# Attention rows loaded in three pieces, zero-padded queries loaded in place, and a longer first lead

## The chip, the cores and the metric

The kernel runs on one core of a Trainium2 chip. The metric is the device time of one execution in microseconds (us). PE is the matrix engine (TensorE), PEld its weight loads, DVE the vector engine, ACT the scalar engine, POOL the GpSimd engine, SP the engine that issues nearly all DMAs here. A name followed by q (SPq, ACTq) is an engine's queue of instructions.

## The reference, cut to what matters

```python
# q, k, v: (4 batches, 8 heads, 576 positions, 64), float32
scores = scale * q @ k.T                                  # per batch and head
Dmat   = where(i >= j, gamma[h] ** (i - j), 0)            # decay mask, gamma[h] = 1 - 2**(-5 - h)
x      = (scores * Dmat) @ v                              # to (2304 tokens, 512)
h      = x @ w_in                                         # dense layer, 512 -> 2048
x      = (h * sigmoid(1.702 * h)) @ w_out                 # 2048 -> 512
expert = argmax(normalised x . normalised expert_emb / tau)   # one of 8 experts per token
out    = gate * relu(x @ w1[expert]) @ w2[expert]         # 512 -> 1024 -> 512
```

## The kernel before

Three stages follow one another: attention (to about 79 us of the profiled span), the dense layer on six blocks of 384 tokens (to about 490 us), and the experts. Only attention and the first microseconds of the dense layer are touched.

**Tiling of attention.** Two heads make a pair; 4 batches by 4 pairs give 16 pairs `bp`. A pair's 576 positions are four chunks of 128 and a tail of 64, so 80 steps `(bp, ch)` in all, `ch` 4 being the tail. A recurrent state `kvs` carries what earlier chunks contribute: within a step PE computes the scores of the chunk (L298, or L301 for the tail), adds the chunk to the state (L325; ACT scales it out of PSUM in L327), and forms the output from the state (L341, from chunk 1 on) and from the masked scores `pr` (L345). DVE multiplies scores by the mask (`pr`, L303) and the finished output by a decay (`keep`, L363 and L360).

**Data of a pair.** `att[bp]` is one row buffer of 128 partitions by 2048 floats (1 MB): columns 0 to AK=512 are the keys transposed (K), AK to AV=1024 the keys in natural order, AV to AQ=1536 the values, AQ to AW=2048 the queries. There are five row buffers (`NBUF`). The matmuls read the queries from a tile `qz` (four of them, `NQ`), in which each head's queries stand in its own 64 partitions and the other 64 partitions are zero; the zeros are written once at the start (L278). `tails[b]` holds, for the four pairs of a batch, the tail's keys, queries and values (384 KB). `tab` holds masks and decays.

**`load(bp)`** issues the whole row as one DMA on SP, for the first batch also the pair's table, and for the first pair of a batch the tails. Pair 0 alone is different: its queries go straight from DRAM into `qz[0]` beside the zeros, in two DMAs, one for each head, and its other columns come over ACT's queue in two pieces.

**`prep(bp)`** makes a loaded pair ready on POOL: it copies the queries of each head from the row into `qz` (L310, not for pair 0), scales the natural keys by a decay (L313; on DVE for pair 0), and copies the tail's queries from `tails` into `qz` (L316, two copies).

**Order.** The instruction order is written out by hand. Odd and even pairs alternate step by step: `turns[0]` are the even pairs' steps, `turns[1]` the odd ones'. The first three steps of pair 0 go ahead, then one odd step and one even step in turn. At step i the loop issues: `prep(bp + 2)` when ch is 0; the scores of step i + 2; state and output of step i; `keep` when ch is 3 or 4; and, when ch is 4, `load(bp + 5)` into the buffer that pair `bp` leaves. At three of these places a first-layer weight unit `wd` (1 MB) is loaded too, and after the last row the constants and more `wd` units. SP issues in program order, and a DMA that waits for a buffer holds back those behind it.

**Weight conversion.** The dense weights come as 64-bit floats; a generator `convert()` turns unit after unit into two 32-bit words: ACT takes the magnitude (L165), DVE does two passes of about 0.7 us (L178, L180) and two of 1.2 us (L185, L192), ACT copies the high word (L168), and DVE subtracts it (`low`, L172). The generator yields a cost after each DVE piece. From attention step 37 on each step calls `flush()` (issue postponed ACT pieces) and `pull(0.23)` (issue pieces until that budget is spent; the overdraft is carried on as `debt`). In the dense layer `swish` pulls 2.6 within each step.

**Dense start.** The order of the first dense matmul groups on PE is h0 and h1 (unit 0 on token blocks 0 and 1), h2 (unit 1, block 0), then the second layer of h0, and so on.

Of the kernel before, what the change touches and what calls it, by code (L numbers as in the profile page):

```python
# [17 lines left out]
P = 128  # L18
B, H, S, HD = 4, 8, 576, 64
NPAIR = H // 2  # L20
NCH = 4
TAIL = S - NCH * P
# [19 lines left out]
RING = 12  # L42
BIG = 100000.0
LAG = 2
WARM = 34
HOLD = NF1 - LAG - 1 - KD
STOP = 1000.0
WD_AT = (7, 11, 14)
NWD = 3
NBUF, NQ = 5, 4  # L50
# [4 lines left out]
AK, AV, AQ, AW = NCH * P, 2 * NCH * P, 3 * NCH * P, 4 * NCH * P  # L55
TQ, TV, TAW = TAIL, 2 * TAIL, 3 * TAIL
# [18 lines left out]
def retention_moe_kernel(  # L75
# [18 lines left out]
    PE, ACT, DVE, POOL, SP = nc.tensor, nc.scalar, nc.vector, nc.gpsimd, nc.sync  # L94
# [26 lines left out]
    def unit_tile(name, shape, dt, s):  # L121
        return pool.tile(shape, dt, tag=f"unit{s % NF1}", bufs=1, name=name)
# [8 lines left out]
    def load_wd(u):  # L131

        t = unit_tile(f"wd{u}", [P, 2048], I32, HELD + u)
        stg["d", u] = t.rearrange("p (n two) -> p n two", two=2)
        SP.dma_start(t, wd[u].bitcast(I32))
# [6 lines left out]
    def load_due():  # L142

        if st.get("loaded"):
            while due:
                load_wd(due.pop(0))

    def flush(*keys):
        for k in keys or list(later):
            if k in later:  # L150
                later.pop(k)()
# [74 lines left out]
    def slot(name):  # L226
        st["slots"] = st.get("slots", -1) + 1
        assert st["slots"] < HELD
        return unit_tile(name, [P, 2048], F32, st["slots"])

    def attention():
        psum = tc.tile_pool(name="psum_a", bufs=1, space=bass.MemoryType.PSUM, reuse_waits="tile")
        with psum as psum:
            yield from attention_(psum)

    def attention_(psum):


        row = [slot(f"row{i}") for i in range(1, NBUF)]
        row.insert(0, slot("row0"))  # L240
        qz = [slot(f"qz{i}") if i > 1 else pool.tile([P, 2048], F32, tag="tab", bufs=2, name=f"qz{i}") for i in range(NQ)]
        tb = slot("tb")[:, : NPAIR * TW].rearrange("p (n w) -> p n w", w=TW)
        ends = slot("ends")
        tl = [ends[:, NPAIR * TAW * i : NPAIR * TAW * (i + 1)].rearrange("p (n w) -> p n w", w=TAW) for i in range(2)]
# [3 lines left out]
        x0[0], x0[1] = x0_tile(0), x0_tile(1)  # L248
        NBP = B * NPAIR

        def load(bp):
            t = row[bp % NBUF]
            b, pair = divmod(bp, NPAIR)
            if bp:
                SP.dma_start(t, att[bp])
            else:
                for j in range(2):
                    r = slice(64 * j, 64 * j + 64)
                    SP.dma_start(qz[0][r, S * j : S * j + NCH * P], att[bp, r, AQ:])
                ACT.dma_start(t[:, :AK], att[bp, :, :AK])  # L260
            if b == 0:
                SP.dma_start(tb[:, bp], tab[:, bp])
            if bp == 0:
                ACT.dma_start(t[:, AK:AQ], att[bp, :, AK:AQ])
            if pair == 0:
                SP.dma_start(tl[b % 2], tails[b])

        load(0)
        DVE.memset(ones, 1.0)
        ACT.copy(scr, ones[:, :16])  # L270

        warm = psum.tile([P, 512], F32, tag="o", bufs=2, name="warm")
        for _ in range(WARM):
            PE.matmul(warm[:, :P], ones, ones, start=True, stop=True)
        scs = [psum.tile([P, 512], F32, name=f"sc{i}") for i in range(3)]
        for i in range(NQ):
# [2 lines left out]

            if i < 3:  # L280
                DVE.memset(scs[i][:, : 2 * P], 0.0)
        for bp in range(1, NBUF):
            load(bp)
        POOL.memset(cum, 0.0)

        def scores(n):
# [16 lines left out]
            DVE.tensor_tensor(pr[:, :, :w], sc[:, :, :w], mask[:, :, :w], ALU.mult)  # L303

        def prep(bp):
            t, end = row[bp % NBUF], tl[bp // NPAIR % 2][:, bp % NPAIR, TQ:TV]
            for j in range(2):
                r, q0 = slice(64 * j, 64 * j + 64), S * j
                if bp:
                    POOL.tensor_copy(qz[bp % NQ][r, q0 : q0 + NCH * P], t[r, AQ:])  # L310
            kd = t[:, AK:AV].rearrange("p (c e) -> p c e", e=HD)
            dec = tb[:, bp % NPAIR, TD + P : TD + P + 2 * NCH]
            (POOL if bp else DVE).tensor_tensor(kd, kd, dec.unsqueeze(2).to_broadcast(kd.shape), ALU.mult)  # L313
            for j in range(2):
                r, q0 = slice(64 * j, 64 * j + 64), S * j + NCH * P
                POOL.tensor_copy(qz[bp % NQ][r, q0 : q0 + TAIL], end[r])  # L316

        def state(bp, ch):
            t = row[bp % NBUF]
# [58 lines left out]


        turns = [[(bp, ch) for bp in range(p, NBP, 2) for ch in range(NCH + 1)] for p in range(2)]  # L380
        steps = turns[0][:3]
        for a, b in zip(turns[1], turns[0][3:] + [None] * 3):
            steps += [a, b] if b else [a]
        prep(0)
        prep(1)
        scores(0)
        scores(1)
        for i, (bp, ch) in enumerate(steps):
            if ch == 0 and bp + 2 < NBP:
                prep(bp + 2)  # L390
            if i + 2 < len(steps):
                scores(i + 2)
            if ch < NCH:
                state(bp, ch)
            chunk(bp, ch)
            if ch >= NCH - 1:
                keep(bp, ch == NCH)
            if ch == NCH:
                if bp + NBUF < NBP:
                    load(bp + NBUF)  # L400
                if bp + NBUF in WD_AT:
                    load_wd(WD_AT.index(bp + NBUF))
                if bp + NBUF + 1 == NBP:

                    st["loaded"] = True
                    SP.dma_start(c[:, :CET], cst[:, :CET])
                    SP.dma_start(c[:, CET : CET + KD * E], embt)
                    uf = pool.tile([P, P], F32, tag="cvb", bufs=1, name="uf")
                    SP.dma_start(uf, cst[:, CU:CSL])
                    load_due()  # L410
            yield
# [458 lines left out]
    def pull(us):  # L870

        k = 0
        us += debt.pop()
        while us > 0 and k < len(bg):
            cost = next(bg[k], None)
            if cost is None:
                bg.pop(k)
            elif cost == STOP:
                k += 1
                us -= 0.7  # L880
            else:
                us -= cost
        debt.append(min(us, 0.0))

    bg.append(convert())
    for i, _ in enumerate(attention()):
        if i > 36:
            flush()
            pull(0.23)
    psum = ctx.enter_context(tc.tile_pool(name="psum", bufs=1, space=bass.MemoryType.PSUM, reuse_waits="tile"))  # L890

    def fill_slots():
# [17 lines left out]
    steps = [(blk, f) for f in range(NF1) for blk in range(2)]  # L910
# [126 lines left out]
    for i in range(nd - 1):  # L1037
# [15 lines left out]
        else:  # L1053
# [4 lines left out]
            if blk < NB - 1 and f == 6:  # L1058
                split_x0(blk + 1)
        if i >= LAG:  # L1060
            dense2(i - LAG)
            u = i - LAG - (nd - NF1)
            if u == 0:
# [7 lines left out]
    while bg:  # L1071
        pull(STOP)
    for f in range(LAG + 1):
        dense2(nd - LAG - 1 + f)
    last = last_rows()
# [185 lines left out]
```

## Time and profile before

| | |
|---|---|
| three runs | 725.32, 726.46, 727.14 us; median 726.46 |
| the profiled execution | 726.2 us; its span, first to last instruction, 724.4 us |
| busy share of the span | PE 97%, PEld 91%, DVE 64%, ACT 42%, POOL 31% |
| DMA | 113.86 MB, 157 GB/s over the span |
| mean granted clock of PE | 0.997 |

All stretches and starts are microseconds from the start of the span. A PE that is busy without a gap is taken as bound by itself; the idle time of another engine costs nothing as long as PE does not wait for it. In a timeline row the first number is the start, the second the duration, and what stands in brackets is the idle time before it and what ended it.

### The profile page before, as it was taken

The page shows a single profiled execution, that of the slowest core. Times are in us where ns is not written, and L with a number is a line of the kernel's source. Part 1 is how long each engine was busy: PE and PEld are TensorE (multiplying, and loading weights), DVE is VectorE, ACT ScalarE, POOL GpSimd, SP SyncE. Part 2 cuts the span into 40 slices and gives each one's busy share as a digit, 9 for nine tenths or more (in the row PEclk, how much of TensorE's full clock was granted, in tenths as well). Part 3 has the DMA queues.
Part 4 walks back from the last instruction along what each step waited for, and adds up shares of the span by engine and source line. Part 5 has one row for each costly group of instructions (what it writes and reads, how often), then busy time and mean ns, then how long its engine had stood idle before and what let it go on. Part 6 is the DMA issues. An engine that isn't in the chain of part 4 may idle for free. (4 is left out here: it accounts for less than half of the span.)

```text
span 724.4 us, 13776 instructions
## 1 busy us (share of the span) xinstructions
PE 704.7 (97%) x5118; PEld 658.2 (91%) x5118; DVE 464.6 (64%) x1085; ACT 306.9 (42%) x586; POOL 227.3 (31%) x251
## 2 busy tenths in 40 slices
PE   7998999999999999999999999999999999999994
PEld 6988898998998998899899899989999999999994
DVE  4788788888636887674476468656564563564561
ACT  1553354544455323332332243353445545555542
POOL 4998000000000221220111102223347457466553
PEclk9999999999999999999999999999999999999998
DMA  9998999300130012200400321144678989888761
GB/s 330 373 359 306 357 356 368 84 1 0 65 114 0 1 56 76 89 1 1 132 1 1 91 84 59 59 142 129 203 188 267 238 250 265 229 267 260 241 185 61
DMA packets 53030, 113.86 MB, mean 157 GB/s; under 512 B 8146, under 2 KB 29010, under 8 KB 48736
## 3 DMA queue, kind: packets, MB, share of 16 engines
q1 hardware_dynamic: 49472, 102.71, 44.2%
q0 software_dynamic: 3200, 9.46, 3.7%
q8 instruction: 41, 0.67, 0.4%
q10 hardware_dynamic: 288, 0.79, 0.4%
q14 instruction: 29, 0.24, 0.1%
HBM read 85.09 MB, written 28.17 MB: 156 GB/s over the span
## 5 line engine op out<-in xcount | busy, mean ns | idle before, releaser
L459 PE MATMUL h<-x,unit 128*128 128x384 f32 x1152 | 217.6, 337 | 1.3 <-DVE unit L172 1.0
L459 PEld LDWEIGHTS h<-x,unit 128*128 128x128 f32 x1152 | 204.6, 188 | 9.9 <-DVE unit L172 1.3
L218 POOL TENSOR_TENSOR unit<-we,unit 128x512 fp32r<-128x512 f32 x64 | 102.4, 1607 | 116.8 <-ACT unit L216 98.5
L459 PE MATMUL eh<-xt,unit 128*128 128x336 f32 (+6 forms) x672 | 102.1, 301 | 0.2 <-DVE eg54l L504 0.2
L459 PEld LDWEIGHTS eh<-xt,unit 128*128 128x128 f32 x672 | 95.4, 188 | 0.9 <-DVE eg54l L504 0.5
L217 DVE TENSOR_TENSOR unit<-we,unit 128x512 fp32r<-128x512 f32 x64 | 56.3, 880 | 61.7 <-ACT unit L216 61.1
L216 ACT CAST unit<-we 128x1024 fp32r<-128x1024 f32 x64 | 66.8, 1046 | 27.0 <-DMA we<-we 25.5
L566 DVE CUSTOM_DVE_ANT_0 dj<-xr,en 128x512 bf16<-128x512 f32 x120 | 78.1, 698 | 0.0
L532 POOL TENSOR_TENSOR enrm<-scr,c 128x8 f32<-128x8 f32 x1 | 1.7, 1687 | 150.4 <-ACT ej L537 150.4
L298 PE MATMUL sc<-qz,row 128*64 128x128 f32 (+1 forms) x512 | 40.0, 259 | 6.4 <-issue 2.3
L303 DVE TENSOR_TENSOR pr<-sc,tb 128x256 f32<-128x256 f32 (+1 forms) x80 | 30.6, 392 | 13.8 <-PE sc L298 11.3
L298 PEld LDWEIGHTS sc<-qz,row 128*64 128x64 f32 x512 | 31.3, 145 | 8.3 <-issue 2.9
L327 ACT ACTIVATE ends<-s,tb 128x64 f32<-128x64 f32 x64 | 19.8, 314 | 35.5 <-PE s L325 32.8
L509 POOL DMA_INDIRECT out<-y,idx x24 | 24.5, 1021 | 32.0 <-ACT y L732 21.5
L345 PE MATMUL ao<-pr,row 128*64 128x128 f32 x256 | 31.1, 283 | 0.9 <-DVE pr L303 0.8
L509 POOL DMA_INDIRECT xs<-xr,slot x18 | 19.4, 1078 | 39.1 <-DVE xr L641 35.7
L626 POOL TENSOR_TENSOR cum<-cum,oh_all 128x8 bf16<-128x8 bf16 x18 | 4.9, 275 | 67.0 <-PE rk L619 65.6
L325 PE MATMUL s<-row 128*64 128x64 f32 x256 | 24.3, 229 | 0.4 <-ACT ends L327 0.4
L341 PE MATMUL ao<-qz,ends 128*64 128x128 f32 x192 | 23.4, 280 | 0.1
L345 PEld LDWEIGHTS ao<-pr,row 128*64 128x64 f32 x256 | 20.6, 142 | 2.1 <-DVE pr L303 2.0
L432 POOL TENSOR_TENSOR x<-x0s,x 128x768 fp32r<-128x768 f32 x3 | 6.1, 2049 | 48.7 <-ACT x L431 48.7
L172 DVE TENSOR_TENSOR unit<-ca,unit 128x1024 fp32r<-128x1024 f32 x16 | 19.6, 1223 | 2.8 <-ACT unit L168 2.8
(1303 smaller groups left out, 1567.1 us busy)
## 6 DMA issues: line engine op xcount, KB each, us to landing
we<-we SPq DMA_DIRECT2D x64, 512.0 KB, 4.4
wd<-wd SPq DMA_DIRECT2D x16, 1024.0 KB, 10.3
row<-att SPq DMA_DIRECT2D x15, 1024.0 KB, 7.3
xs<-fill SPq DMA_DIRECT2D x22, 257.0 KB, 11.2
xrow<-xr SPq DMA_DIRECT2D x18, 257.0 KB, 3.8
y<-yd SPq DMA_DIRECT2D x7, 512.0 KB, 4.5
x0d<-x0f SPq DMA_DIRECT2D x4, 768.0 KB, 11.2
x0s<-x0d SPq DMA_DIRECT2D x8, 384.0 KB, 6.9
```

Of the source, the lines that this page charges most:

```text
L216: ACT.copy(w[:, 0, :], t)
L217: DVE.tensor_tensor(w[:, 1, :512], t[:, :512], w[:, 0, :512].bitcast(F32), ALU.subtract)
L218: POOL.tensor_tensor(w[:, 1, 512:], t[:, 512:], w[:, 0, 512:].bitcast(F32), ALU.subtract)
L298: PE.matmul(sc[64 * i : 64 * i + 64, j, q0:], t[:, k0 : k0 + 64], q[j][:, q0:P], start=True, stop=True)
L303: DVE.tensor_tensor(pr[:, :, :w], sc[:, :, :w], mask[:, :, :w], ALU.mult)
L325: PE.matmul(s[64 * j : 64 * j + 64], t[:, AK + c0 : AK + c0 + 64], t[:, AV + c0 : AV + c0 + 64], start=ch == 0, stop=True, skip_group_chec ...
L327: ACT.activation(kvs[bp % 2][:, 64 * ch : 64 * ch + 64], s, AF.Copy, scale=tb[:, bp % NPAIR, dec : dec + 1])
L341: PE.matmul(o[64 * j : 64 * j + 64], kvs[bp % 2][:, 64 * (ch - 1) : 64 * ch], qz[bp % NQ][:, q0 : q0 + n], start=True, stop=False)
L345: PE.matmul(o[64 * j : 64 * j + 64], v, pr[:, j, :n], start=ch == 0, stop=True)
L459: PE.matmul(h, w[:, a, P * dc : P * (dc + 1)], xt[:, b, dc, :n], start=k == 0, stop=k == len(terms) - 1)
L509: i = POOL.indirect_dma_start(out=dst[:, :], out_offset=bass.IndirectOffsetOnAxis(ap=rows, axis=0), in_=src, in_offset=None, bounds_check= ...
L566: DVE.tensor_tensor_reduce(junk, r[:, :D], en[e // 4][:, e % 4, :], 1.0, 0.0, ALU.mult, ALU.add, dots[:, E * k + e : E * k + e + 1])
```

## The change

- `LEAD = 4`: the first four steps of pair 0, its whole run of full chunks, go ahead of the first odd step instead of three. Elsewhere this shifts the two interleaved sequences against each other by one step, and leaves the last four steps of pair 15 alone at the end instead of three.
- `load` takes a column range. For pairs 5 to 15 the row comes in three DMAs, issued at different steps of the pair that leaves the buffer: the queries at its chunk 0, K at its chunk 3, natural keys and values at its tail.
- The queries of pairs 0 and 1 go into `qz` beside the zeros, two DMAs each; pair 1 needs no L310 any more.
- The tail's queries of every pair go from DRAM into `qz` by two DMAs (`load_ends`, 64 partitions by 256 bytes each), in place of POOL's L316. For pairs 4 to 15 they are issued after the tail step of the pair that leaves the `qz` tile.
- The order of the initial loads on SP becomes: queries 0, table 0, queries 1, K and keys and values of row 1, table 1, ends 0, tails 0, ends 1, then rows 2 to 4 whole, each with its table and ends (2 and 3), then tails 1. Before, tails 0 came ahead of row 1.
- After attention, ahead of the dense layer, `flush()` and `pull(2.4)`: conversion pieces that were issued within the first `swish` are issued before it.

```diff
+LEAD = 4
-        def load(bp):
-            t = row[bp % NBUF]
-            b, pair = divmod(bp, NPAIR)
-            if bp:
-                SP.dma_start(t, att[bp])
-            else:
+        def load(bp, lo, hi, q=SP):
+            if lo == AQ and bp < 2:
                 for j in range(2):
                     r = slice(64 * j, 64 * j + 64)
-                    SP.dma_start(qz[0][r, S * j : S * j + NCH * P], att[bp, r, AQ:])
...
+                    SP.dma_start(qz[bp][r, S * j : S * j + NCH * P], att[bp, r, AQ:])
+                return
+            q.dma_start(row[bp % NBUF][:, lo:hi], att[bp, :, lo:hi])
...
+        def load_ends(bp):
+
+            b, pair = divmod(bp, NPAIR)
+            for j in range(2):
+                r, q0 = slice(64 * j, 64 * j + 64), S * j + NCH * P
+                SP.dma_start(qz[bp % NQ][r, q0 : q0 + TAIL], tails[b, r, pair, TQ:TV])
+
+        load(0, AQ, AW)
+        load(0, 0, AK, ACT)
+        load_tab(0)
+        load(0, AK, AQ, ACT)
...
-        for bp in range(1, NBUF):
-            load(bp)
+        load(1, AQ, AW)
+        load(1, 0, AQ)
+        load_tab(1)
+        load_ends(0)
+        load_tails(0)
+        load_ends(1)
+        for bp in range(2, NBUF):
+            load(bp, 0, AW)
+            if bp < NPAIR:
+                load_tab(bp)
+            if bp < NQ:
+                load_ends(bp)
+        load_tails(1)
...
-                if bp:
+                if bp > 1:
                     POOL.tensor_copy(qz[bp % NQ][r, q0 : q0 + NCH * P], t[r, AQ:])
...
-            for j in range(2):
-                r, q0 = slice(64 * j, 64 * j + 64), S * j + NCH * P
-                POOL.tensor_copy(qz[bp % NQ][r, q0 : q0 + TAIL], end[r])
...
-        steps = turns[0][:3]
-        for a, b in zip(turns[1], turns[0][3:] + [None] * 3):
+        steps = turns[0][:LEAD]
+        for a, b in zip(turns[1], turns[0][LEAD:] + [None] * LEAD):
...
         for i, (bp, ch) in enumerate(steps):
+            nxt = bp + NBUF
             if ch == 0 and bp + 2 < NBP:
                 prep(bp + 2)
+            if nxt < NBP and ch in (0, NCH - 1):
+                load(nxt, *((0, AK) if ch else (AQ, AW)))
             if i + 2 < len(steps):
                 scores(i + 2)
...
             if ch == NCH:
-                if bp + NBUF < NBP:
-                    load(bp + NBUF)
...
+                if nxt < NBP:
+                    load(nxt, AK, AQ)
+                if bp + NQ < NBP:
+                    load_ends(bp + NQ)
+                if nxt < NBP and nxt % NPAIR == 0:
+                    load_tails(nxt // NPAIR)
+                if nxt in WD_AT:
+                    load_wd(WD_AT.index(nxt))
...
             pull(0.23)
+    flush()
+    pull(2.4)
```

## Rows read from the trace of the kernel before

**Rows 1.** Busy time by stretch: us, engines' busy us (instructions), PE clock, DMA share, GB/s.

```profile
0.00:10.00 10.00, 6.98 (x66) 6.07 (x66) 5.99 (x14) 1.78 (x3) 1.84 (x9) 1.00 0.80 265
10.00:20.00 10.00, 7.94 (x128) 7.47 (x129) 3.33 (x9) 2.23 (x8) 7.64 (x14) 1.00 1.02 408
20.00:30.00 10.00, 10.00 (x242) 10.00 (x240) 7.33 (x19) 5.31 (x18) 9.31 (x17) 1.00 0.96 351
...
40.00:50.00 10.00, 8.56 (x187) 7.81 (x185) 8.28 (x16) 5.51 (x14) 9.37 (x15) 1.00 0.94 342
...
```

**Rows 2.** What PE waited for, 0 to 92 us: total, times, longest.

```profile
PE sc L298 <- issue: 2.3, 2, 1.6
PE sc L298 <- POOL qz L310: 2.1, 1, 2.1
PE sc L298 <- DMA qz<-att: 2.0, 2, 1.3
```

**Rows 3.** PE's timeline at the start: start, duration, line, operation.

```profile
12.16 1.36 PE L298 MATMUL sc<-qz,row 128*64 128x128 f32 x8 [2.06 <-POOL qz L310]
...
14.17 1.05 PE L298 MATMUL sc<-qz,row 128*64 128x128 f32 x8
...
15.87 1.05 PE L298 MATMUL sc<-qz,row 128*64 128x128 f32 x8
...
18.69 0.39 PE L298 MATMUL sc<-qz,row 128*64 128x128 f32 x6
```

**Rows 4.** POOL's timeline, the query copies of pairs 1 and 2.

```profile
11.50 1.27 POOL L310 COPY qz<-row 64x512 f32<-64x512 f32 x2 [2.02 <-DMA row<-att]
...
14.55 1.28 POOL L310 COPY qz<-row 64x512 f32<-64x512 f32 x2 [0.18 <-DMA row<-att]
```

**Rows 5.** ACT's timeline: one state read of the repeating pattern, first and last.

```profile
18.45 0.31 ACT L327 ACTIVATE ends<-s,tb 128x64 f32<-128x64 f32 x1 [0.57 <-PE s L325]
...
40.62 0.32 ACT L327 ACTIVATE ends<-s,tb 128x64 f32<-128x64 f32 x1 [0.57 <-PE s L325]
```

**Rows 6.** POOL's instructions by line and shape, 42 to 72 us.

```profile
L310 POOL COPY qz<-row 64x512 f32<-64x512 f32 x14 | 9.4, 669 | 1.3 <-DMA row<-att 0.7
L313 POOL TENSOR_TENSOR row<-row,tb 128x512 f32<-128x512 f32 x7 | 8.2, 1164 | 0.6
L316 POOL COPY qz<-ends 64x64 f32<-64x64 f32 x14 | 7.2, 513 | 0.4
```

**Rows 7.** DVE's timeline: a conversion pass within attention, and the dense start.

```profile
43.73 1.52 DVE L178 TENSOR_SCALAR ca<-ca 128x1024 f32<-128x1024 f32 x1 [1.38 <-ACT ca L165]
...
80.31 0.22 DVE L412 CAST ub<-uf 128x128 bf16<-128x128 f32 x1
82.63 0.56 DVE L492 SCALAR_TENSOR_TENSOR g0t<-g0t,h 128x384 f32<-128x384 f32 x1 [2.10 <-ACT g0t L490]
```

**Rows 8.** DVE's instructions by line and shape, 42 to 80 us.

```profile
L178 DVE TENSOR_SCALAR ca<-ca 128x1024 f32<-128x1024 f32 x3 | 2.9, 963 | 1.4 <-ACT ca L165 1.4
```

**Rows 9.** The same view, 82 to 130 us, in the dense layer.

```profile
L185 DVE SCALAR_TENSOR_TENSOR ca<-wd,ca 128x1024 int32<-128x1024 int32 x7 | 8.6, 1224 | 0.2
...
L178 DVE TENSOR_SCALAR ca<-ca 128x1024 f32<-128x1024 f32 x6 | 4.1, 689 | 2.1 <-ACT ca L165 2.1
```

**Rows 10.** PE's timeline at the end of attention and the start of the dense layer.

```profile
79.12 0.29 PE L345 MATMUL at<-pr,ends 128*64 128x64 f32 x4
...
85.50 2.03 PE L459 MATMUL h<-x,unit 128*128 128x384 f32 x10 [1.01 <-DVE unit L172]
```

**Rows 11.** Busy time by stretch: first loads; 8 KB rows; 2 KB rows. Columns as Rows 1.

```profile
2.00:5.50 3.50, 2.87 (x27) 2.62 (x26) 2.85 (x7) 1.12 (x2) 0.00 (x0) 1.00 0.94 276
86.00:90.00 4.00, 4.00 (x22) 3.61 (x21) 3.48 (x6) 1.94 (x3) 0.00 (x0) 1.00 1.02 427
119.00:124.00 5.00, 5.00 (x28) 4.61 (x27) 4.40 (x6) 2.55 (x4) 0.00 (x0) 1.00 1.03 397
```

**Rows 12.** DMA queue from 64 to 65 us: packets, MB, share of 16 engines.

```profile
q1 hardware_dynamic: 404, 0.40, 119.2%
```

More of the change, by code (lines that the diff above doesn't have):

```diff
@@ L249, in attention_, with load_tab, load_tails @@
         NBP = B * NPAIR
-        def load(bp):
-            t = row[bp % NBUF]
-            b, pair = divmod(bp, NPAIR)
-            if bp:
-                SP.dma_start(t, att[bp])
-            else:
+        def load(bp, lo, hi, q=SP):
+            if lo == AQ and bp < 2:
                 for j in range(2):
                     r = slice(64 * j, 64 * j + 64)
-                    SP.dma_start(qz[0][r, S * j : S * j + NCH * P], att[bp, r, AQ:])
[L260 to L268, printed above, removed]
+                    SP.dma_start(qz[bp][r, S * j : S * j + NCH * P], att[bp, r, AQ:])
+                return
+            q.dma_start(row[bp % NBUF][:, lo:hi], att[bp, :, lo:hi])
+        def load_tab(bp):
+            SP.dma_start(tb[:, bp], tab[:, bp])
+        def load_tails(b):
+            SP.dma_start(tl[b % 2], tails[b])
+        def load_ends(bp):
[7 more added lines that the diff above has]
+        load(0, AK, AQ, ACT)
         DVE.memset(ones, 1.0)
@@ L305, in prep @@
         def prep(bp):
-            t, end = row[bp % NBUF], tl[bp // NPAIR % 2][:, bp % NPAIR, TQ:TV]
+            t = row[bp % NBUF]
             for j in range(2):
                 r, q0 = slice(64 * j, 64 * j + 64), S * j
-                if bp:
+                if bp > 1:
                     POOL.tensor_copy(qz[bp % NQ][r, q0 : q0 + NCH * P], t[r, AQ:])
@@ L398, in attention_ @@
             if ch == NCH:
-                if bp + NBUF < NBP:
-                    load(bp + NBUF)
-                if bp + NBUF in WD_AT:
-                    load_wd(WD_AT.index(bp + NBUF))
-                if bp + NBUF + 1 == NBP:
+                if nxt < NBP:
[6 more added lines that the diff above has]
+                    load_wd(WD_AT.index(nxt))
+                if nxt + 1 == NBP:
                     st["loaded"] = True
```

## The prediction

> **What bounds the kernel now.** I read the table by stretches first, to find where PE is not busy. It idles 3.0 us in the first 10 us and 2.1 us in the next, not at all from 20 to 40, 1.4 us from 40 to 50 [rows 1]. In the dense layer it is busy in the whole of 86 to 90 [rows 11], and so in nearly every stretch up to 690 us. So PE sets the time, and a microsecond that attention ends earlier is a microsecond off the total, as no stage between waits for anything but PE. DMA is at a share near 1 in the same stretches of attention [rows 1]: data are a second limit, and a transfer that is put ahead pushes back another.
>
> PE's list of waits names the gaps [rows 2]. 2.0 us for the first queries are not touched: the loads in front of them stay. 2.1 us go to pair 1's query copy on POOL, whose row landed at 11.5 us [rows 4]; pair 0 still had a full chunk to do, but its scores stand behind pair 1's in PE's order. 1.0 us goes to unit 1 of the dense weights [rows 10]. 2.3 us are two stops inside a group of eight matmuls, for which the profile names no releaser.
>
> [...] And ACT's pattern, which recurs once per pair of five steps, gives the steady pace: six periods from 18.45 to 40.62 [rows 5], 3.70 us a pair or 0.74 us a step. At 40.62 there are 44 steps left, 32.5 us at that pace, to 73.1; attention's last matmul ends at 79.41 [rows 10]. So 6.3 us are lost there: 2.3 in the two stops, 4.0 elsewhere, and these are DVE's. From step 37 it has, for ten steps, eight masks of 0.42, two of 0.29, two `keep`s of 0.69 + 0.21 and conversion of 2.3 by its budget: 8.0 us against PE's 7.4.
>
> **Part 1, the start (pairs 0 and 1 in place, new order of loads, LEAD 4).** Removed: pair 1's two copies and the wait for tails 0 ahead of its row. Row 1 landed at 11.50 with 2630 KB issued up to its end and row 2 at 14.55 with 3852 KB [rows 4]: 1222 KB in 3.05 us, 410 GB/s, in order of issue. With 2246 KB up to row 1's K and values it lands near 10.6; allowing 0.2 us for the smaller pieces, 10.8. PE leaves its first chunk at 10.1 and now has pair 0's next full step, 1.70 us at the slow level [rows 3], so pair 1's scores are asked for at 11.8 and are there: the gap of 2.06 us goes.
>
> But it comes back in part two pairs on, and here I name what is late next. The bytes ahead of row 2 are the old ones plus 64 KB of ends in 256 small packets: it lands at 14.55 + 0.15 + 0.25 = 14.95 (price of the packets below), then POOL copies each half of its queries in 0.64 us, to 16.2. PE arrives at pair 2's scores between 14.8 and 16.1, as the clock rises early or late, so row 2 decides, not the clock. Before, these scores stood at 18.69 [rows 3]; now at 16.3. Of these 2.4 us one step of 0.74 is still owed, since LEAD 4 puts pair 2 a step earlier in the order. **Gain 1.6**, from 1.0 (row 2 later by 0.6) to 2.1.
>
> Next in line is POOL. From 15 us on it has per pair of batches 0 and 1 1.27 + 1.04 + about 1.1 (low halves), which is under PE's pace, but it starts at row 2's landing, and pairs 4 and 6 are needed two steps earlier against it than before. My count of its queue puts pair 6's copies 0.3 us late. **Cost 0.3**, from 0 to 1.0.
>
> **Part 2, rows in pieces.** Keys and values still wait for the output matmul of chunk 3 of the old pair, as the whole row did; only queries (by eight steps) and K (by a step and a half) go earlier. In steady state no one waits for rows, so the gain is counted at nothing. SP issues three loads and two ends for one load, four more at 0.35 to 0.5 us each, under 2 us a pair against 3.70: its waiting covers that. The new wait is that of the ends for the tail step of the pair that leaves the `qz` tile; behind it on SP stand the next pair's K and the `wd` loads, held for two steps at most, 1.5 us. POOL, which needs them, comes nine steps later. In the first pairs the ends and tails 0 land near 12.3, the tail's scores are due at 13.5.
>
> The price in DMA time: rows of 2 KB ran at 397 GB/s against 427 for 8 KB [rows 11], which makes a row in pieces about 0.15 us longer. A slice with 384 packets of 128 to 792 bytes and some 0.22 MB of 8 KB rows took 1.0 to 1.2 us [rows 12]; the 8 KB part takes 0.52 of that, so a small packet costs an engine 20 to 28 ns, and a pair's 128 ends, eight an engine, 0.2 us. Together 0.35 us a pair. Between rows 5 and 15 the queue carries 3.94 MB besides (three `wd`, two tails), 0.84 us a row; 0.84 + 2.65 + 0.2 is just PE's 3.70. **Counted at 0**, because a lead of about 4 us (row 5 should be there at 26 and is needed at 30) covers a deficit; the other end is a rival.
>
> **Part 3, L316 gone.** 7.2 of POOL's 24.8 us in these three lines from 42 to 72 us are the ends' copies [rows 6]. That is off PE's path, but DVE's conversion passes stop behind POOL: L178 took 1.52 us at 43.73 [rows 7], with POOL's L313 running in the same time, and its three in attention 0.96 each [rows 8] against 0.69 in the dense layer, where POOL rests [rows 9]. L178 is the first of five such pairs of groups; over them the eleven passes take 12.7 us against 10.3 uncontended, so 2.4 us in a stage that DVE bounds. With POOL busy for 0.71 of the time I take the same share of the collisions away, 0.7, rounded down. **Gain 0.6**, from 0 to 2.4.
>
> **Part 4, four lone steps at the end.** A lone step waits for its own state on ACT; the last two show 0.28 us each on the weight loads. One more: **cost 0.2**, from 0.1 to 0.3.
>
> **Part 5, the pull.** The budget carried over is 43 x 0.23 less the pieces' costs, -0.23, so 2.17 buys L185 of unit 2 and `low` of unit 1, 1.22 us each [rows 9]. They fill DVE's 2.10 us between 80.53 and the first swish at 82.63 [rows 7]. Unit 1 is then ready at 83.0, h2 is due at 84.5: the gap of 1.01 us before 85.50 goes [rows 10]. Late next: the first swish by 0.34, and its low half, behind L192 and the two passes of unit 3 that the pull of 2.6 now reaches, at about 87.15, where PE wants it at 87.0. **Gain 0.8**, from 0.4 to 1.0.
>
> **Sum.** 1.6 - 0.3 + 0 + 0.6 - 0.2 + 0.8 = 2.5 us, from the profiled execution's 726.2: 723.7 us. That execution lies 0.3 under the median, 726.46. What a measurement of this kernel tells from no change is 0.3%, 2.2 us: faster is under 724.3, slower over 728.6.
>
> **The rivals.**
>
> *A, the start gives it back.* The pieces ahead of row 2 go at the rate of the first loads, 276 GB/s [rows 11], 0.4 us more, POOL's delay is its upper bound 1.0, and part 3 is nothing: 1.2 - 1.0 - 0.2 + 0.8 = 0.8, **725.4**. For it: DMA share 1.02 from 10 to 20 [rows 1], so nothing can be pulled in without pushing something out. Against: the 410 GB/s of the same stretch.
>
> *B, the unnamed stops go too.* 2.3 us more [rows 2], **721.4**. For it: they stand at places in the run of instructions that the new order moves, and DMA was nearly full at both. Against: nothing in the change removes a cause that I can name.
>
> *C, slower: transfers become the bound.* The place is SP's queue of rows 5 to 15. What is left of PE's pace for a row is 2.65 us; with the lead of 4 us over 11 rows 3.0, so it decides where pieces fall under about 350 GB/s. At the 276 GB/s of the first loads, which were pieces of 2 and 4 KB as well [rows 11], a row takes 3.8 us, 11 x 1.15 - 4 = 8.6 us lost: 726.2 - 2.5 + 8.6 = **732**. Against: the first loads include the ramp from an idle queue, and the 2 KB rows at 397 were in full flow. [...]
>
> *D, uneven DVE.* With the sequences shifted, the `keep`s of an odd and an even pair fall within six steps of ten, 4.3 us of DVE work in 4.4 before any conversion piece, then four light ones. If that makes the loss of 4.0 us half again as large, **725.7**. Against: DVE is bound over the whole ten steps either way.
>
> **Chances.** The forecast 0.48, its own range 722.6 to 724.8; A 0.18, B 0.12, C 0.10, D 0.12. Faster: four fifths of the forecast's, all of B and a little of A, 0.52; slower: C and a remainder, 0.11; same 0.37. The range 721.2 to 727.4 leaves out C and the far side of B.
>
> **What would show it.** Right: PE without a wait near 10 to 12, pair 2's scores near 16.3 with a wait before them of up to 1.5 us for POOL's copy; 3.70 us a pair until 40; the conversion passes nearer their uncontended times; attention ending near 77.7; no wait before h2. Wrong: PE waiting for row DMAs after 25 (C); longer gaps after masks than before (D); a start no earlier than 17.5 for pair 2 (A).

## The result, and the profile after

The changed kernel takes 734.82 us, median of six executions (733.18 to 736.91), beside 726.55 for the kernel before, six executions on the same chip: ratio 1.0115, 95% interval 1.0095 to 1.0134. It is slower by 8.3 us, where 723.7 was forecast. The profiled execution took 733.18 us, the fastest of the six, with a span of 731.4 against 724.4; so the trace accounts for 7.0 us, and what the slower executions lose besides has no trace.

The view by stretches shows where. Columns as in [rows 1]; the last two rows are finer stretches, where PE comes back after its stop.

```profile
50.00:60.00 10.00, 3.02 (x48) 2.73 (x46) 2.54 (x7) 1.86 (x5) 5.67 (x8) 0.77 1.01 359
60.00:70.00 10.00, 10.00 (x216) 9.94 (x214) 8.07 (x19) 3.97 (x11) 6.10 (x7) 0.89 0.71 238
```

```profile
58.00:60.00 2.00, 1.73 (x20) 1.73 (x22) 0.00 (x0) 0.53 (x3) 0.24 (x1) 0.50 1.04 371
60.00:62.00 2.00, 2.00 (x31) 2.00 (x29) 0.85 (x3) 0.47 (x2) 0.80 (x1) 0.50 0.94 335
```

From 50 to 60 us PE works 3.02 us of ten, and the granted clock is below full in that stretch and the next: it is 0.50 from 56 to 62 us.

In the list of PE's waits, beside [rows 2], the wait for ACT's state reads has grown from 0.4 us to 7.2:

```profile
PE s L341 <- ACT ends L343: 7.2, 3, 6.7
PE sc L317 <- POOL qz L329: 2.1, 3, 1.6
...
PE sc L317 <- DMA row<-att: 1.0, 1, 1.0
```

PE waits 6.7 us at one place for a state that ACT reads. ACT's timeline says why the state is late, and PE's what follows:

```profile
56.89 1.12 ACT L166 ACTIVATE ca<-wd 128x1024 f32<-128x1024 f32 x1 [6.67 <-DMA wd<-wd]
57.91 0.31 ACT L343 ACTIVATE ends<-s,tb 128x64 f32<-128x64 f32 x1
```

```profile
58.27 0.48 PE L341 MATMUL s<-row 128*64 128x64 f32 x4 [6.72 <-ACT ends L343]
...
59.39 0.85 PE L317 MATMUL sc<-qz,row 128*64 128x128 f32 x8
...
62.34 0.50 PE L317 MATMUL sc<-qz,row 128*64 128x128 f32 x8
...
86.06 0.29 PE L361 MATMUL at<-pr,ends 128*64 128x64 f32 x4
```

The magnitude pass of the second dense unit (L166) stands in ACT's order ahead of attention's next state read (L343). Its weights, `wd` 1, had not landed, so ACT stopped for 6.67 us, and PE with it. The granted clock had fallen while PE stood still: 0.87 from 54 to 56 us, 0.50 from 56 to 58, with no matmul in either. When PE came back, eight score matmuls took 0.85 us at a clock of 0.50; from 62.34 on they take 0.50 us again, and the clock is 1.00 from 63 to 70 us. The 4.07 us from 58.27 to 62.34 would be 2.4 us at the ratio of these two rows, so the stop cost 6.7 + 1.7 = 8.4 us on the spot. At the end of attention 6.94 us of it are left: its last matmul ends at 86.35, against 79.41 [rows 10], nearly the whole difference of the spans. That it is less than 8.4 is in part because the kernel before has two unnamed stops of its own, 2.3 us [rows 2], which the list of the changed kernel does not have.

The load itself is in SP's timeline, first of the changed kernel and then of the kernel before:

```profile
47.90 1.11 SPq L271 DMA_DIRECT2D qz<-tails  x2
49.45 0.33 SPq L136 DMA_DIRECT2D wd<-wd  x1
```

```profile
40.52 0.43 SPq L135 DMA_DIRECT2D wd<-wd  x1
```

And this is SP's list of waits from 14 to 80 us, in the same order:

```profile
SPq L271 <- DMA row<-att: 7.7, 10, 2.2
...
SPq L258 <- DMA row<-att: 5.5, 7, 2.2
```

```profile
SPq L255 <- PE ao L345: 30.9, 10, 3.8
SPq L135 <- PE ao L345: 14.9, 5, 5.2
```

`wd` 1 was issued at 49.45; before, at 40.52. The kernel before waits on SP in this stretch for engines alone, that is for buffers to come free. In the changed one the ends' loads (L271) wait 7.7 us for *rows*, which they neither read nor write. The landings in the trace tell what they wait for. Up to 80 us no load of SP was issued, in either kernel, before the eighth load ahead of it (the two of ACT at the start counted) had landed, and in the changed one 29 of 84 were issued within 0.1 us of that landing. Three of them, in us:

| load | issued | the eighth ahead of it | issued | landed |
|---|---|---|---|---|
| a row piece of 256 KB (L258) | 45.78 | a row piece of 512 KB (L258) | 39.37 | 45.77 |
| `wd` 1 (L136) | 49.45 | a row piece of 512 KB (L258) | 44.12 | 49.44 |
| ends, 16 KB (L271) | 52.13 | a row piece of 256 KB (L258) | 46.95 | 52.07 |

So at most eight loads were under way at a time. With one load a pair eight loads are eight rows, more than there are buffers; with five they are 1.6 pairs, and a piece of 16 KB held its place nearly as long as the one of 512 KB, 5.05 us (44.58 to 49.63) beside 5.32.

At both ends of the change the first step came as forecast. PE's and POOL's timelines at the start, beside [rows 3, 4]:

```profile
12.55 0.34 PE L320 MATMUL sc<-qz,ends 128*64 128x64 f32 x4 [0.38 <-DMA ends<-tails]
...
15.72 0.43 PE L317 MATMUL sc<-qz,row 128*64 128x128 f32 x4 [1.61 <-POOL qz L329]
16.39 0.43 PE L317 MATMUL sc<-qz,row 128*64 128x128 f32 x4 [0.24 <-POOL qz L329]
```

```profile
15.06 1.27 POOL L329 COPY qz<-row 64x512 f32<-64x512 f32 x2 [2.73 <-DMA row<-att]
...
19.48 1.27 POOL L329 COPY qz<-row 64x512 f32<-64x512 f32 x2 [2.02 <-DMA row<-att]
...
23.33 1.27 POOL L329 COPY qz<-row 64x512 f32<-64x512 f32 x2
...
25.69 1.55 POOL L390 TENSOR_TENSOR x<-x,x 128x384 fp32r<-128x384 f32 x2
27.18 1.28 POOL L329 COPY qz<-row 64x512 f32<-64x512 f32 x2
```

The wait for pair 1's copy is gone, and pair 2's scores stand at 15.72 and 16.39. But from 23.33 to 27.18 POOL needs 3.85 us for a pair, not less than PE's 3.70 [rows 5].

And at the dense start, beside [rows 7, 10], PE, then DVE:

```profile
93.78 0.51 PE L493 MATMUL o<-unit,g0l 128*128 128x512 f32 x1 [0.35 <-DVE g0l L520]
...
111.50 0.51 PE L493 MATMUL o<-unit,g4l 128*128 128x512 f32 x1 [0.72 <-DVE g4l L520]
```

```profile
108.29 0.70 DVE L179 TENSOR_SCALAR ca<-ca 128x1024 f32<-128x1024 f32 x1 [1.60 <-ACT ca L166]
109.02 0.69 DVE L181 TENSOR_SCALAR ca<-ca 128x1024 int32<-128x1024 int32 x1
109.75 1.23 DVE L186 SCALAR_TENSOR_TENSOR ca<-wd,ca 128x1024 int32<-128x1024 int32 x1
110.89 0.55 DVE L520 TENSOR_TENSOR g4l<-g4t,g4h 128x384 fp32r<-128x384 f32 x1
```

The wait of 1.01 us before the second hidden unit is gone. A wait of 0.35 for the first low half has come, and one of 0.72 at the fifth unit, whose low half stands behind three conversion passes and their wait for ACT.

### The profile page after: what moved, and what is told of

Read it like the earlier page. It is cut to its first block, busy times and chain, and to the rows that moved or that the text cites. A ratio compares the mean times of both kernels' runs of the same rounds, so it can differ in the third digit from the quotient of the medians.

```text
span 731.4 us, 13847 instructions
## 1 busy us (share of the span) xinstructions
PE 705.2 (96%) x5118; PEld 658.4 (90%) x5118; DVE 460.7 (63%) x1085; ACT 306.2 (42%) x586; POOL 216.9 (30%) x217
## 5 line engine op out<-in xcount | busy, mean ns | idle before, releaser
L218 DVE TENSOR_TENSOR unit<-we,unit 128x512 fp32r<-128x512 f32 x64 | 54.5, 852 | 61.2 <-ACT unit L217 61.1
L317 PE MATMUL sc<-qz,row 128*64 128x128 f32 (+1 forms) x512 | 36.9, 256 | 5.3 <-POOL qz L329 2.1
L343 ACT ACTIVATE ends<-s,tb 128x64 f32<-128x64 f32 x64 | 19.9, 312 | 34.0 <-PE s L341 33.2
L341 PE MATMUL s<-row 128*64 128x64 f32 x256 | 21.8, 231 | 7.7 <-ACT ends L343 7.2
L361 PE MATMUL ao<-pr,row 128*64 128x128 f32 x256 | 28.7, 285 | 0.3
L341 PEld LDWEIGHTS s<-row 128*64 128x64 f32 x256 | 17.1, 144 | 9.0 <-ACT ends L343 7.9
L332 POOL TENSOR_TENSOR row<-row,tb 128x512 f32<-128x512 f32 x15 | 17.0, 1134 | 21.9 <-DMA row<-att 11.9
L166 ACT ACTIVATE ca<-wd 128x1024 f32<-128x1024 f32 x16 | 18.4, 1147 | 8.0 <-DMA wd<-wd 6.7
```

Of the source, the lines that this page charges most:

```text
L218: DVE.tensor_tensor(w[:, 1, :512], t[:, :512], w[:, 0, :512].bitcast(F32), ALU.subtract)
L317: PE.matmul(sc[64 * i : 64 * i + 64, j, q0:], t[:, k0 : k0 + 64], q[j][:, q0:P], start=True, stop=True)
L341: PE.matmul(s[64 * j : 64 * j + 64], t[:, AK + c0 : AK + c0 + 64], t[:, AV + c0 : AV + c0 + 64], start=ch == 0, stop=True, skip_group_chec ...
L343: ACT.activation(kvs[bp % 2][:, 64 * ch : 64 * ch + 64], s, AF.Copy, scale=tb[:, bp % NPAIR, dec : dec + 1])
L361: PE.matmul(o[64 * j : 64 * j + 64], v, pr[:, j, :n], start=ch == 0, stop=True)
```

## The experiments

Three theories stood at first: T1, the number of loads under way on SP; R1, the bytes and packets of the pieces; R2, that `wd` is held behind the ends' wait for the tail step. Ratios are to the kernel before on the same chip, with 95% intervals.

**The ends copied by POOL again** (three loads a pair).

```diff
-                if bp + NQ < NBP:
-                    load_ends(bp + NQ)
...
+                POOL.tensor_copy(qz[bp % NQ][r, q0 : q0 + TAIL], end[r])   # in prep
```

> The changed kernel with the tail's queries copied by POOL again, as before, and no DMA for them: three loads a pair on SP instead of five. Three theories of why ACT waited 6.7 us for the second dense weight unit. T1, too many loads in flight: every load on SP waits until the eighth load before it has landed, so five a pair at some 6 us each need 3.75 us a pair against PE's 3.70, and SP falls behind. R1, bytes: the 256-byte and 2 KB packets are slow. R2, held back: the new loads of the ends wait for the tail step and hold the weight unit behind them. T1: the stop goes, with some 1.7 us of PE at the low clock after it, 733.2 to about 725. R1: only the ends' packets go, 731 to 733. R2: also about 725, this run does not tell it from T1.

727.7 us, 1.0029 (1.0011 to 1.0048). `wd` 1 is issued at 42.80 and ACT waits 0.26 us for it. The main loss is gone. What is left over the kernel before is not taken apart; PE waits 2.6 us, six times, for query copies, so more than the 2.1 us that the start was to save [rows 2] is lost to POOL again.

**The same ends' loads from POOL's own queue.**

```diff
-                SP.dma_start(qz[bp % NQ][r, q0 : q0 + TAIL], tails[b, r, pair, TQ:TV])
+                POOL.dma_start(qz[bp % NQ][r, q0 : q0 + TAIL], tails[b, r, pair, TQ:TV])
```

> The changed kernel with the same loads of the ends, same bytes and same packets, issued by POOL on its own queue, so that SP has three loads a pair. T1 (count in flight on SP's queue): the stop goes, about 725 to 727, POOL paying for the issue. R1 (packets and bytes): all packets are still there, 732 to 735. R2 (held behind the wait for the tail step): the wait is off SP, 725.

734.43 us, 1.0125 (1.0108 to 1.0142). That is R1's number and not T1's, but not for R1's reason: with all the packets still there, ACT's wait fell from 6.67 to 1.77 us, as T1 says. The time is lost elsewhere, for issuing a load kept POOL busy for 0.55 us. POOL by line from 14 to 80 us, and a stretch of all engines:

```profile
L271 POOL DMA_DIRECT2D qz<-tails x24 | 13.2, 552 | 0.0
```

```profile
30.00:40.00 10.00, 8.22 (x155) 7.59 (x152) 4.73 (x13) 3.50 (x11) 9.71 (x15) 0.86 1.04 392
```

POOL is busy 9.71 us of ten, and PE waits 5.6 us for query copies (2.1 in the changed kernel). The engine that was to be relieved spends 13.2 us on 24 loads; in the kernel before the 30 copies of the same stretch took it 10.9.

**Rows 5 to 15 whole, the ends on SP with their waits** (three loads a pair).

```diff
-            if nxt < NBP and ch in (0, NCH - 1):
-                load(nxt, *((0, AK) if ch else (AQ, AW)))
...
-                    load(nxt, AK, AQ)
+                    load(nxt, 0, AW)
```

> The changed kernel with rows 5 to 15 as one load each at the tail step, as before, and the ends still loaded by SP behind their wait for the tail step: three loads a pair. T1: SP keeps up, the stop goes, 725 to 726. R1: the 2 KB pieces go and the ends' packets stay, 728 to 732. R2: the weight unit still stands behind the ends' wait, the stop stays, 731 to 734.

726.67 us, 1.0012 (0.9999 to 1.0026); `wd` 1 issued at 42.93, ACT's wait 0.17 us. The ends' wait for the tail step is still ahead of `wd`, so R2 falls.

**The second weights asked for two pairs earlier.**

```diff
-WD_AT = (7, 11, 14)
+WD_AT = (7, 9, 14)
```

> The changed kernel with the second dense weight unit loaded two pairs earlier in SP's order, nothing else. If ACT's wait for it is all that was lost, 733.2 - 6.7 - about 1.7 us of low clock = 725. If SP's lateness (T1) goes on and only the first victim is gone, rows 11 to 14 land late instead and PE waits for them: 727 to 731. R1 the same as T1 here.

730.96 us, 1.0078 (1.0061 to 1.0095). `wd` 1 is there in time, and now ACT, and PE behind it, stops for the third unit:

```profile
72.18 1.12 ACT L166 ACTIVATE ca<-wd 128x1024 f32<-128x1024 f32 x1 [3.57 <-DMA wd<-wd]
```

Rows are about as late as in the changed kernel: POOL waits 13.6 us for their keys from 14 to 80 us, there 11.9, and in the kernel before not at all. Here another order of the queue changed who waits, and did not end the lateness.

**The kernel before with four 16 KB loads more a pair, or one of 64 KB.** Their bytes go to columns that nobody reads (`spare`, the rest of buffers whose first columns attention fills), and no engine is waited for.

```diff
                     load(bp + NBUF)
+                    for k in range(4):
+                        r, q0 = slice(64 * (k % 2), 64 * (k % 2) + 64), NT - 2 * TB + 64 * ((2 * bp + k // 2) % 8)
+                        SP.dma_start(spare[bp // 4][r, q0 : q0 + 64], tails[bp // NPAIR, r, bp % NPAIR, TQ:TV])
```

> The kernel before, with four loads of 16 KB more on SP behind each of the rows 5 to 15, into columns that nothing reads: five loads a pair as in the changed kernel, but rows whole, nothing waiting for the small ones and no wait for another engine added. The theory that the number of loads on SP is what costs (eight may be under way, so the ninth waits for the first of them): SP gets waits on DMA of 5 us or more (none in the kernel before), and the loads of the dense weights land later than before by 2 us or more; whether PE then stops is a question of their lead, 727 to 731. The theory of bytes and packets: 0.4 us of DMA time a pair, SP's waits stay on engines, time within 1 us of 726.5.

```diff
                     load(bp + NBUF)
+                    q0 = NT - 2 * TB + 128 * (bp % 4)
+                    SP.dma_start(spare[bp // 4][:, q0 : q0 + 128], tails[bp // NPAIR, :, bp % NPAIR, :TV])
```

> The twin: the same 64 KB a pair in one load more instead of four, so two loads a pair. Theory of the number: SP has under 1 us of waits on DMA, second weights at most 1 us later, time 726 to 727. Theory of bytes: the same as with four small loads, within 0.5 us.

Four: 732.31 us, 1.0084 (1.0056 to 1.0112). One: 727.28, 1.0000 (0.9983 to 1.0018). SP's waits, ACT's second magnitude pass and PE's wait with four:

```profile
SPq L405 <- DMA row<-att: 9.1, 6, 2.8
...
SPq L135 <- DMA row<-att: 2.7, 1, 2.7
```

```profile
53.75 1.13 ACT L165 ACTIVATE ca<-wd 128x1024 f32<-128x1024 f32 x1 [5.15 <-DMA wd<-wd]
```

```profile
55.13 0.48 PE L343 MATMUL at<-qz,ends 128*64 128x64 f32 x4 [4.68 <-ACT ends L329]
```

and with one, SP's largest wait (none in its list is for a DMA) and the same pass:

```profile
SPq L257 <- PE ao L347: 24.5, 10, 3.5
```

```profile
50.09 1.19 ACT L165 ACTIVATE ca<-wd 128x1024 f32<-128x1024 f32 x1 [0.86 <-DMA wd<-wd]
```

This pair settles it. The same 64 KB cost nothing that could be measured in one load; in four they make the kernel before stop for the same pass of ACT as the changed one, with whole rows, no new wait for an engine and no other part of the change. The two differ in packets too, 256 of 256 bytes against 128 of 512 a pair. That these aren't it is shown by the ends over POOL's queue, where all packets of the changed kernel are still there and ACT's wait is 1.77 us, and by the whole rows, with 128 packets of 256 bytes a pair and a wait of 0.17. R1 falls.

**The changed kernel with a row in two pieces** (queries, then keys and values: four loads a pair).

```diff
-                load(nxt, *((0, AK) if ch else (AQ, AW)))
+                load(nxt, AQ, AW) if ch == 0 else None
...
-                    load(nxt, AK, AQ)
+                    load(nxt, 0, AQ)
```

> The changed kernel with a row in two pieces (queries at the new pair's first step, keys and values together where values were): four loads a pair instead of five. By the number of loads on SP: with eight under way a load waits for the one two pairs before it, against 1.6 pairs with five and 2.7 with three (second dense weights awaited 6.7 us with five, 0.2 to 0.3 with three): ACT waits 1 to 4 us for them, time 728 to 731. Rival, that it is the pieces of 16 KB as such: between three and five loads nothing changes before the ends go, wait 5 us or more, 733.

730.77 us, 1.0054 (1.0034 to 1.0073):

```profile
53.10 1.13 ACT L166 ACTIVATE ca<-wd 128x1024 f32<-128x1024 f32 x1 [2.34 <-DMA wd<-wd]
```

ACT's wait for `wd` 1 by loads a pair: 6.67 us (five, the change), 5.15 (five, small ones added), 2.34 (four), 0.17 to 1.33 (three, in five kernels; 1.77 in the one with POOL's queue), 0.86 (two), 0 to 1.67 (one, in five kernels). These are single profiles: up to three loads they scatter between 0 and 1.8, from four on the wait rises.

**The pull alone, and a smaller one.** Part 5 in the kernel before, with 2.4 and with 1.3.

```diff
             pull(0.23)
+    flush()
+    pull(2.4)      # or pull(1.3)
```

> The kernel before with the one line that drains more conversion pieces behind attention and nothing else. Part 5 of the prediction said 0.8 us (0.4 to 1.0); by the two profiles the stretch from attention's end to the third hidden unit was 0.66 us shorter. Right: 725.6 to 726.1 beside 726.5, the wait of 1.0 us before the second hidden unit gone, one of 0.3 to 0.4 for a low half in its place. Rival: unit 2's pieces hold back the first swish and nothing is gained, 726.5.

> The kernel before with a smaller pull behind attention, one conversion piece instead of two, so that no unit has three passes that begin with the clamp (which waits for ACT's magnitude pass) ahead of its low half. If the second unit's wait of 1.0 us goes and no wait at the fifth takes its place: 0.5 to 0.9 us under the kernel before in the profile between attention's end and the seventh unit. Rival: DVE's passes are the bound of that stretch, the wait only moves, 0.3 us or less.

2.4: 726.71 us, 0.9994 (0.9977 to 1.0012). From the dense layer's first matmul to the hidden unit behind its first output group it takes 9.05 us instead of 9.73, but the fifth unit's wait of 0.75 us comes as in the changed kernel, and the step there takes 5.2 us instead of 4.2. Over these steps together it takes 26.78 us instead of 26.45. 1.3: 725.59, 0.9987 (0.9975 to 0.9999), and 25.54 us over the same steps. Neither wait appears:

```profile
79.57 6.68 PE L459 MATMUL h<-x,unit 128*128 128x384 f32 x36 [0.31 <-DVE x0f L363]
...
105.11 2.27 PE L459 MATMUL h<-x,unit 128*128 128x384 f32 x12
```

One piece moved ahead is enough. In DVE's order no three passes that begin with the wait for ACT then stand ahead of a low half at these steps. That this is the reason is not shown: in the kernel before three such passes stand ahead of the fourth unit's low half, from 96.80 us, and PE does not wait there.

**The start and the pull, rows whole, ends copied** (one load a pair): the changed kernel with the diffs of the first and third experiments together.

> The changed kernel with rows 5 to 15 whole and the ends copied by POOL again: start, order of the first loads, four chunks ahead, and the pull remain; one load a pair. If all the loss lies in the number of loads, SP has no waits on DMA and the gains of the start (1.4 us by the keep times of pairs 2 to 6) and of the pull (0.7) show: 724.3 to 725. If the start's gain is given back by POOL's lateness for pairs 4 and 6, as the two half-undone kernels' profiles suggest, only the pull is left: 725.5 to 726.5. If four chunks ahead costs by itself, 726.5 to 728.

728.73 us, 1.0015 (1.0000 to 1.0029). With the loads' number as before, the kernel is still not faster. In its timeline POOL takes 4.44 us a pair from 21.88 to 35.19 (copy 1.28, scaling 1.04, ends 0.52, low halves 1.55), and pairs 2, 4 and 6 wait for it (2.3 us in six waits).

**Whole rows, ends in place, no pull; four and three chunks ahead; the start alone.** The first is the third experiment without the pull, the second has `LEAD = 3` besides, and the last has the ends copied as well.

> The changed kernel with rows 5 to 15 whole and without the pull: what remains is the start, the ends loaded in place and four chunks ahead. In the kernel before with the pull alone, the 0.67 us that the first units gain are lost again at the fifth unit, whose low half stands behind three conversion passes. If so here: the wait of 1.0 us before the second hidden unit is back, no wait for the low half of the fifth unit, and the time is the same as with whole rows and the pull (726.7) within 0.5 us. Rival: the pull was worth 0.7 us there, 727.4. By attention's end (78.1 us with whole rows and the pull, 79.7 before) 1.5 us of gain should stand, 725 to 725.5, unless executions differ by as much.

> The same with three chunks ahead, as in the kernel before. Theory that POOL's queue paces the first two batches (1.28 + 1.04 + 1.55 = 3.87 us a pair, and POOL starts with row 2): pair 2's scores stand a step later in the order, so POOL's waits of PE for pairs 2, 4 and 6 shrink by up to 0.7 us each in the first case, but what comes out at 40 us is POOL's own pace, so the end of attention moves by under 0.4 us; 0.5 us either way in the total. Rival, that four ahead costs by itself (lone steps at the end, uneven work of DVE): 0.5 to 1.5 us faster than with four ahead.

> The start alone (queries of pairs 0 and 1 in place, new order of the first loads), three chunks ahead, whole rows, ends copied by POOL, no pull. POOL then needs 1.28 + 1.04 + 0.52 + 1.55 = 4.4 us a pair in the first two batches against PE's 3.7, without the ends' copies 3.9. Theory that POOL's queue gives the start's gain back: the gain of 1.4 us at pair 0 is gone by pair 6, and the time is that of the kernel before, 726 to 726.8. Rival, that the start by itself makes the gain that the kernel with the ends in place showed (0.9979): 724.7 to 725.3.

Four ahead: 726.08 us, 0.9990 (0.9978 to 1.0002). Three ahead: 724.86, 0.9979 (0.9966 to 0.9991), the fastest kernel here; the 1.2 us between the two are what the rival said, but the intervals overlap. The start alone: 726.05, 1.0011 (0.9995 to 1.0027), the time of the kernel before, as its theory has it. With three ahead, taking the ends off POOL parts 0.9979 from 1.0011, and these intervals, measured on two chips, just don't overlap. With four ahead and the pull it parts 1.0012 from 1.0015, which is no difference.

**The fastest with the smaller pull.**

```diff
             pull(0.23)
+    flush()
+    pull(1.3)
```

> The start, ends in place, whole rows and three chunks ahead (724.9, 0.9979 of the kernel before), with the pull of one piece (0.9987 by itself) behind attention. If the two gains lie in different stretches and add up: 0.9966, 724 to 724.5 beside 726.5, no wait before the second hidden unit. Rival: with attention's end earlier the conversion is behind again, a wait of 0.3 to 0.8 us for a low half takes the place, and the time is that without the pull.

725.49 us, 0.9989 (0.9976 to 1.0003). No wait for a low half appears, so the rival's mechanism isn't there, but the gains don't show as a sum either. Single profiles of the kernels with the new start and whole rows end attention anywhere from 77.7 to 81.5 us, with unnamed stops that come and go, so what lies between 0.998 and 1.000 is not told apart here.

## Why the prediction was wrong, step by step

**Rows in pieces (part 2): the step that failed.** It said of SP's four loads more that "its waiting covers that", counting 0.35 to 0.5 us of issue each, and that `wd` is held "two steps at most, 1.5 us" with POOL coming nine steps later. It missed two things. A load on SP also waited for the eighth before it (`wd` 1 at 49.45 for a landing at 49.44), so the number of loads, not the time to issue them, limited how far SP ran ahead; from 14 to 80 us SP's waits on DMA, none before, come to 17.7 us. And the first that needs `wd` 1 is not POOL but ACT, whose order puts the magnitude pass ahead of the state that PE waits for. Counted at nothing, it cost 8.4 us on the spot: 6.7 of stop and 1.7 at the clock of 0.50 after it. The four small loads in the kernel before show the cause by itself. The limit could have been read from the trace of the kernel before: there SP waits 4.2 us for row loads in the first 24 us, and row 3 is issued at 7.13, right after the eighth load before it (with ACT's two counted) had landed, at 7.11. In the changed start, with ends and queries in between, the same row is issued at 12.39. Before, then after:

```profile
7.13 0.33 SPq L255 DMA_DIRECT2D row<-att  x1
```

```profile
12.39 0.58 SPq L258 DMA_DIRECT2D row<-att  x1
```

**Rival C** had the sign and the size, 732, but not the mechanism. It priced bytes and pieces, up to 276 GB/s; from 20 to 50 us, after and then before, the queue's packets, bytes and busy share were

```profile
q1 hardware_dynamic: 4413, 9.28, 90.0%
```

```profile
q1 hardware_dynamic: 1602, 10.78, 95.6%
```

less busy and with fewer bytes, which is SP not issuing. PE's own wait for row transfers after 25 us, which was to show C, is 1.0 us. Of A only the delay at POOL came true, about 1.2 of the start's 1.4 us; its sign, a start of pair 2 no earlier than 17.5, did not show. B's two stops are indeed gone from the changed kernel's list, but such stops come and go between profiles (1.7 us with the ends copied, none named in the pull alone), so that is no proof that the change removed them. D can't be read beside a stop of 6.7 us.

**The start (part 1).** Right in its steps: row 2 at 15.06 (14.95), pair 2's scores around 16 (16.3), a wait of 1.61 + 0.24 (up to 1.5, so a little longer). For the kernel before, the clock column shows 1.00 in every stretch of 2 us from 0 to 18, although the score matmuls take about twice their later time until 16.7 (1.05 us for eight, then 0.39 for six) [rows 3], so the level there rests on the matmuls' rows alone. In the changed kernel the column has the rise: 0.50 from 8 to 10 us, where eight score matmuls take 0.85, 0.73 from 10 to 12 and 1.00 from 12 on, where they take 0.54 (13.24). The `keep` of pair 2 came at 23.23 instead of 25.38, 1.4 us earlier when the owed step of 0.74 is taken off. The "cost 0.3" for POOL was mis-sized: "about 1.1" for its low halves is the mean over batches 0 and 1, but the pairs of batch 0 take 1.55 us and come first. So POOL needs 3.85 us a pair there and is over PE's pace, not under it. It was so before, too, with 4.45 us a pair (20.50 to 24.95), hidden by its lead:

```profile
24.95 1.55 POOL L374 TENSOR_TENSOR x<-x,x 128x384 fp32r<-128x384 f32 x2
```

And row 3, issued late, was there only at 19.48. At pair 6, whose `keep` came at 39.27 against 40.19, 0.2 us of the 1.4 were left; the rest went to POOL's pace and the late row. The start alone measures no gain.

**L316 gone (part 3).** The mechanism shows: the ten conversion passes inside attention take 10.4 us instead of 12.0. But there the stop has also moved passes to where POOL is done. Without it, in the two kernels with whole rows and three chunks ahead, they take 10.3 us with the ends loaded and 11.2 with the ends copied, 0.9 us where 0.7 was expected. In the total it shows only in these two, as about 2.3 us; how much of that is the passes', and how much POOL's shorter queue in the first pairs, is not settled. That DVE bounds the stage was worked out from its load and is not shown: up to 92 us PE's list of the kernel before puts 0.8 us down to DVE's masks.

**The lone steps (part 4)**, 0.2 us, are below what these comparisons tell; four ahead against three, 0.9990 and 0.9979, overlap.

**The pull (part 5).** 0.66 of the 0.8 us came, and the low half's wait that was named came too. What was missed is later: 1.0 us is lost at the fifth unit, where the moved passes meet their wait for ACT ahead of a low half. The net in the pull alone is 0.3 us of loss by the profiles, and nothing in the time.

## What to carry to other kernels

At most eight loads were under way here, so a load cost a place among the eight besides its bytes and its issue (four of 16 KB more a pair 1.0084, one of 64 KB 1.0000). Before a transfer is cut into pieces, count how many loads the queue issues in the time of its longest lead, and read the queue's waits for loads that have nothing to do with the waiting one. Look for who needs a late transfer first in *program order*: here ACT, whose order serves two streams, handed a wait of 6.67 us in one on to the other. And when work is moved ahead, follow the waits of the mover for a whole period of its pattern, since here a stop of 1.01 us went at the second hidden unit and one of 0.72 came at the fifth.

## What the runs showed of the hardware

After the stop of 6.72 us in the changed kernel the granted clock stayed at 0.50 for 4 us more (58 to 62) and so added 1.7 us to the stop. It happened also after an unnamed stop in the kernel with the start alone, in PE's timeline and the stretches around it:

```profile
64.32 0.56 PE L313 MATMUL sc<-qz,row 128*64 128x128 f32 x8 [2.08 <-issue]
```

```profile
62.00:64.00 2.00, 0.24 (x4) 0.10 (x1) 1.99 (x4) 0.16 (x1) 1.83 (x5) 1.00 0.93 384
64.00:66.00 2.00, 1.68 (x25) 1.68 (x26) 0.95 (x2) 0.31 (x1) 1.92 (x2) 0.69 1.06 376
66.00:68.00 2.00, 2.00 (x33) 2.00 (x31) 0.95 (x3) 0.06 (x1) 1.75 (x5) 0.50 0.69 269
```

The length of the stop alone does not tell. The one of 1.61 us at 15.72 in the changed kernel was not followed by a fall (1.00 from 16 to 20 us), nor was one of 2.1 between 30 and 40 us in the kernel with `wd` 1 two pairs earlier (1.00 from 30 to 50); but in that same kernel one of 1.64 at 15.91 was followed by score matmuls at 1.03 us for eight (18.33), beside 0.54 before it (13.40) and 0.59 later (21.06). Such a fall more or less may be part of the 3 to 5 us by which executions of the same kernel differ here; that was not tried.

Issuing a load from POOL kept that engine busy for 0.55 us, and two of them took 1.07 us one after the other (at 33.78, the ends over POOL's queue).

POOL's copies and DVE's conversion passes took longer when they ran at the same time. In the kernel before the two copies of a pair's ends take 0.23 us each when no such pass runs, one behind the other, 0.52 together. In the stretch of [rows 6] five of the seven pairs took 0.99 to 1.52 us, each while a conversion pass ran on DVE, and the other two 0.52. The pass took longer as well: L185 took 1.63 us beside them, 1.22 in the dense layer [rows 9]. POOL's rows, and then DVE's:

```profile
33.24 0.52 POOL L316 COPY qz<-ends 64x64 f32<-64x64 f32 x2
...
48.94 1.52 POOL L316 COPY qz<-ends 64x64 f32<-64x64 f32 x2
```

```profile
48.45 1.63 DVE L185 SCALAR_TENSOR_TENSOR ca<-wd,ca 128x1024 int32<-128x1024 int32 x1
```

So the 7.2 us that the prediction read for the copies are right, and more than half of them come from this meeting: at 0.23 us each the fourteen would take 3.2, an estimate.
